# Loading the first keys' weights by rows and ordering the head of a fused attention and Mish kernel anew

## The chip, the cores and the metric

The kernel runs on one core of one Trainium2 chip. The metric is the time of one execution in device microseconds. All times below are microseconds unless marked ns.

## The reference, cut to what matters

```python
def reference(A_x, A_wqkv, A_w_phi, A_wo, B_x, B_w1, B_b1, B_w2):
    def _A_ref(x, wqkv, w_phi, wo):
        B, S, D = x.shape                       # 1, 2048, 512
        H = 32; Dh = D // H                     # Dh = 16
        qkv = (x @ wqkv).reshape(B, S, 3, H, Dh).transpose(2, 0, 3, 1, 4)
        q, k, v = qkv[0], qkv[1], qkv[2]
        pq = jnp.einsum("bhsd,hdf->bhsf", q, w_phi)
        pk = jnp.einsum("bhsd,hdf->bhsf", k, w_phi)
        phi_q = jnp.concatenate([_softmax(pq), _softmax(-pq)], axis=-1)
        phi_k = jnp.concatenate([_softmax(pk), _softmax(-pk)], axis=-1)
        kv = jnp.einsum("bhsf,bhsd->bhfd", phi_k, v)
        z  = jnp.einsum("bhsf->bhf", phi_k)
        num = jnp.einsum("bhqf,bhfd->bhqd", phi_q, kv)
        den = jnp.einsum("bhqf,bhf->bhq", phi_q, z)[..., None] + 1e-6
        return (num / den).transpose(0, 2, 1, 3).reshape(B, S, D) @ wo
    def _B_ref(x, w1, b1, w2):                  # w1: 512 x 1792
        h = jnp.einsum("bsd,df->bsf", x, w1) + b1
        sp = jnp.log1p(jnp.exp(-jnp.abs(h))) + jnp.where(h > 0, h, 0)
        return jnp.einsum("bsf,fd->bsd", h * jnp.tanh(sp), w2)
    x = A_x
    xn = _layernorm(x, axis=-1)
    return x + _A_ref(xn, A_wqkv, A_w_phi, A_wo) + _B_ref(xn, B_w1, B_b1, B_w2)
```

All tensors are bf16. The work is one layer normalisation of 2048 tokens, a linear attention with a learned feature map per head, and a two-layer Mish network, both added to the input.

## The kernel before, in words

The 2048 tokens are 16 tiles of 128, in four groups of four. `w_phi` is folded into the projection weights, so that one matmul of the normalised tokens with the folded weights gives the softmax logits at once. For the keys this fold happens at the very start, in the part here called the head. Everything is issued by one list of steps, `STEPS`, in which each step is a name with arguments: `@3` names a PSUM bank, and `a`, `v`, `p` name ScalarE (ACT), VectorE (DVE) and GpSimd (POOL). Each engine takes its own instructions in the order of the list and waits only for what its operands need. Weights and tokens are loaded by DMAs of SP's queue, two small tensors by ACT's.

The steps of the head are these (tile i of the first group, row block kt of the keys' weights):

- `LS i`, `RS i`, `AZ i`, `TP i`, `TC i`: statistics of token tile i on DVE; its reciprocal root on ACT (two activations, L597 and L598) or POOL (L171 and L172); the normalised tile `xn` on DVE (L176); its transposes on the tensor engine (PE) into `ptr` (L609); and the copy of these to `xnT` (L628).
- `TW kt`, `TK kt`: row block kt of the keys' weights `wkp` is transposed on PE, four blocks of 128 by 128, as plain matmuls with the identity into an fp32 bank `ptw` (L616), and copied to `wT` (L622). Only blocks 0 and 1 go this way; blocks 2 and 3 come already turned, by one DMA transpose out of HBM (L523).
- `WB`: the feature weights `wsrc`, which a DMA of 32-byte pieces lays out, are multiplied with a mask `block` into the block-diagonal `Wbd` on DVE (L568).
- `F0 kt`, `FD kt`: four matmuls of `wT` with `Wbd` into `pfold` (L151), and the copy back to `wkp` (L160).
- `LP i`: logits of token tiles 0 and 1, eight matmuls of 512 columns that take the row blocks in order (L244).
- `PB`, `CB`: the bias turned on PE (L577) and copied on DVE (L669). `KM` builds another mask on DVE (L563). `AM` loads ACT's table for Mish (L139).

Ahead of the steps PE gets twelve warm-up matmuls of ones (L554), nine of 512 columns and three of 128. Behind `LP` come `V t` (values, L229), `VC t` (their copy), `L s i` and `LC s i` (logits of a tile and their copy), `H u` and `M u` (a block of hidden units and its Mish, L263 and L274), `E`, `X`, `S`, `R`, `N`, `A` (softmaxes and accumulation), `LN g` and `AP g k` (normalisation of later groups), `DX g` and `DW i` (later loads).

Of the kernel before, what the change touches and what calls it, by code (L numbers as in the profile page):

```python
# [8 lines left out]
BF16 = mybir.dt.bfloat16  # L9
# [53 lines left out]
def kernel(  # L63
# [13 lines left out]
    P = 128  # L77
# [15 lines left out]
    wphi_v = A_w_phi.rearrange("(j i) a b -> (i a) j b", j=4)  # L93
# [18 lines left out]
    wsrc = wts.tile([P, 4, DH], BF16, name="wsrc")  # L112
    wv = wts.tile([P, KT, D], BF16, name="wv")
# [8 lines left out]
    ident = consts.tile([P, P], BF16, name="ident")  # L122
    mhalf = consts.tile([P, TPG], FP32, name="mhalf")
# [9 lines left out]
    tables = ["natural_log_exp_and_others"]  # L133
# [388 lines left out]
    nc.sync.dma_start(wkp[:, 0:2, :], wqkv_v[:, 0:2, D : 2 * D])
    nc.sync.dma_start_transpose(  # L523
        out=wT_of[0][:, :, 2 * P : 4 * P], in_=A_wqkv[2 * P : 4 * P, D : 2 * D]
    )
# [3 lines left out]
    nc.sync.dma_start(x_sb[:, 2:4, :], x_v[:, 2:4, :])
    nc.sync.dma_start(wv[:], wqkv_v[:, :, 2 * D : 3 * D])  # L530
# [14 lines left out]
    nc.gpsimd.memset(mhalf[:], -0.5)  # L545
    nc.gpsimd.memset(eps[:], 1e-5)
# [20 lines left out]
    def weights_by_block():  # L567
        nc.vector.tensor_tensor(  # L568
            out=Wbd[:].rearrange("p j (h e) -> p j h e", h=8),
            in0=block[:, None, :, :].to_broadcast([P, 4, 8, 16]),  # L570
            in1=wsrc[:, :, None, :].to_broadcast([P, 4, 8, 16]),
            op=ALU.mult,
        )
# [19 lines left out]
    def first_root(i, on):  # L593
        _, mv, rstd = ln_of[0]
        r = rstd[:, i : i + 1]
        if on == "a":
            nc.scalar.activation(r, mv[:, i, 1:2], ACT.Ln, bias=eps[:])  # L597
            nc.scalar.activation(r, r, ACT.Exp, scale=-0.5)  # L598
        else:
            root(r, mv[:, i : i + 1, :])  # L600
# [12 lines left out]
    def turn_keys(kt, b):  # L613
        ptw = pf_of["w", kt] = bank(b, "ptw")
        for j in range(4):
            nc.tensor.matmul(  # L616
# [104 lines left out]
```

## Time and profile before

| | |
|---|---|
| median of 3 runs | 173.61 (173.58 to 173.72) |
| the profiled execution's own time | 173.62 |
| its span, first to last instruction | 171.9 |
| PE busy | 168.3 (98%) |
| DVE busy | 146.0 (85%) |
| ACT busy | 122.2 (71%) |
| POOL busy | 7.9 (5%) |
| mean granted TensorE clock | 1.000 |

Durations and starts in the profile are those of the one profiled execution, counted from the span's start. A row of a timeline gives the start, the time until the last instruction of the row ends, engine, line, operation, output and inputs, and how many such instructions follow each other. In matmul rows the ends are modelled and neighbouring matmuls overlap, so the pace of PE is read from the distance of starts. `PEld` is the loading of weights into PE, and `SPq` and `ACTq` are the instructions that issue DMAs. The granted clock is the share that the throttle grants; it was 1.00 in every slice. The landing time of a DMA counts from the start of its issue.

### The profile page before, as it was taken

The page shows a single profiled execution, that of the slowest core. Times are in us where ns is not written, and L with a number is a line of the kernel's source. Part 1 is how long each engine was busy: PE and PEld are TensorE (multiplying, and loading weights), DVE is VectorE, ACT ScalarE, POOL GpSimd, SP SyncE. Part 2 cuts the span into 40 slices and gives each one's busy share as a digit, 9 for nine tenths or more (in the row PEclk, how much of TensorE's full clock was granted, in tenths as well). Part 3 has the DMA queues.
Part 4 walks back from the last instruction along what each step waited for, and adds up shares of the span by engine and source line. Part 5 has one row for each costly group of instructions (what it writes and reads, how often), then busy time and mean ns, then how long its engine had stood idle before and what let it go on. Part 6 is the DMA issues. An engine that isn't in the chain of part 4 may idle for free.

```text
span 171.9 us, 2743 instructions
## 1 busy us (share of the span) xinstructions
PE 168.3 (98%) x1047; PEld 82.5 (48%) x1047; DVE 146.0 (85%) x226; ACT 122.2 (71%) x196; POOL 7.9 (5%) x23
## 2 busy tenths in 40 slices
PE   8999999999999999999999999999999999999993
PEld 3754444444445544454445644544444444554452
DVE  3769998999899999999989999899799998884333
ACT  2778899976998979799978989978282792432200
POOL 4122102300000000000000000000000000000000
PEclk9999999999999999999999999999999999999999
DMA  4997199686064000000000194309345628778641
GB/s 119 299 374 253 33 217 356 147 162 126 4 115 129 0 4 0 0 0 0 4 0 0 40 111 97 63 15 142 91 107 110 150 59 190 155 161 206 91 124 61
DMA packets 46297, 18.55 MB, mean 108 GB/s; under 512 B 38092, under 2 KB 46284, under 8 KB 46284
## 3 DMA queue, kind: packets, MB, share of 16 engines
q1 hardware_dynamic: 45584, 18.26, 45.8%
q10 hardware_dynamic: 700, 0.12, 0.4%
q8 instruction: 8, 0.13, 0.3%
q14 instruction: 5, 0.04, 0.1%
HBM read 7.10 MB, written 2.10 MB: 53 GB/s over the span
## 4 chain that ended last, share of the span: by engine, by line
PE 98%; DVE 0%; issue 0%
PE ph L263 28%; PE po L497 28%; PE pl L229 14%; PE po L504 8%; PE pv L229 8%; PE warm L554 3%; PE pnd L452 2%; PE pkv L421 2%; PE pl L244 1%; PE pwide L229 1%; PE pfold L151 1%; PE ptw L616 1%; PE ptr L609 1%; PE pfold L203 0%; DVE x_sb L511 0%; PE pb L577 0%
## 5 line engine op out<-in xcount | busy, mean ns | idle before, releaser
L497 PE MATMUL po<-w_sb,acts 128*128 128x512 bf16 (+2 forms) x238 | 50.8, 366 | 0.0
L263 PE MATMUL ph<-xnT,w_sb 128*128 128x512 bf16 x224 | 50.1, 379 | 0.0
L274 ACT ACTIVATE acts<-ph,b1f 128x512 bf16<-128x512 f32 x56 | 35.9, 694 | 5.4 <-PE ph L263 5.4
L340 DVE TENSOR_REDUCE s<-e 128x128 f32<-128x2048 bf16 x16 | 36.1, 2277 | 0.5 <-ACT e L323 0.5
L263 PEld LDWEIGHTS <-w_sb 128*128 128x128 bf16 x224 | 21.7, 98 | 25.9 <-issue 0.3
L497 PEld LDWEIGHTS <-acts 128*128 128x128 bf16 x238 | 22.1, 98 | 23.6
L323 ACT ACTIVATE e<-e 128x2048 bf16<-128x2048 bf16 x16 | 30.4, 1917 | 0.0
L229 PEld LDWEIGHTS <-xnT 128*128 128x128 bf16 x184 | 17.6, 98 | 20.3 <-issue 0.2
L511 DVE TENSOR_TENSOR x_sb<-po,x_sb 128x512 bf16<-128x512 f32 (+2 forms) x17 | 11.0, 656 | 8.4 <-PE po L504 8.4
L504 PE MATMUL po<-wqk,xnT 128*128 128x512 bf16 (+2 forms) x68 | 15.6, 366 | 0.0
L229 PE MATMUL pl<-wqk,xnT 128*128 128x512 bf16 x64 | 15.6, 379 | 0.0
L229 PE MATMUL pv<-wv,xnT 128*128 128x512 bf16 x64 | 15.4, 379 | 0.0
L287 ACT CAST p_sb<-pl 128x512 bf16<-128x512 f32 x21 | 11.9, 590 | 4.1 <-PE pl L229 4.0
L467 ACT COPY ds<-pnd 128x32 f32<-128x32 f32 x16 | 2.9, 183 | 16.5 <-PE pnd L452 16.5
L139 ACT ACT_TABLE_LOAD x10 | 12.8, 1283 | 0.2
L298 DVE TENSOR_TENSOR m<-m 128x512 bf16<-128x512 bf16 (+1 forms) x32 | 11.5, 358 | 1.1
L229 PE MATMUL pl<-wkp,xnT 128*128 128x512 bf16 x48 | 11.5, 379 | 0.0
L165 DVE BATCH_NORM_STATS2 stats<-x_sb 128x6 f32<-128x512 bf16 x16 | 10.1, 678 | 1.3 <-DMA x_sb<-in_A_x_dram 1.3
L298 DVE TENSOR_TENSOR m<-p_sb 128x1024 bf16<-128x1024 bf16 x16 | 10.9, 682 | 0.1
L307 DVE TENSOR_TENSOR e<-p_sb,m 128x2048 bf16<-128x2048 bf16 x8 | 9.8, 1225 | 0.4 <-PE pkv L421 0.2
L374 DVE TENSOR_TENSOR e<-e,r 128x2048 bf16<-128x2048 bf16 x8 | 9.6, 1219 | 0.6 <-ACT r L349 0.5
L307 DVE TENSOR_TENSOR e<-m,p_sb 128x2048 bf16<-128x2048 bf16 x8 | 9.8, 1226 | 0.3
(73 smaller groups left out, 134.0 us busy)
## 6 DMA issues: line engine op xcount, KB each, us to landing
w_sb<-in_B_w_dram SPq DMA_DIRECT2D x4, 896.0 KB, 8.0
out_dram<-x_sb SPq DMA_DIRECT2D x15, 128.0 KB, 2.0
x_sb<-in_A_x_dram SPq DMA_DIRECT2D x3, 512.0 KB, 8.0
wv<-in_A_wqkv_dram SPq DMA_DIRECT2D x1, 512.0 KB, 5.1
wqk<-in_A_wo_dram SPq DMA_DIRECT2D x1, 512.0 KB
x_sb<-in_A_x_dram SPq DMA_DIRECT2D x2, 128.0 KB, 2.1
wkp<-in_A_wqkv_dram SPq DMA_DIRECT2D x1, 256.0 KB, 3.5
x_sb<-in_A_x_dram SPq DMA_DIRECT2D x1, 256.0 KB, 3.5
```

The source lines that it names most:

```text
L139: nc.scalar.preload_act_table_set(name)
L229: nc.tensor.matmul(pp, lhsT=xnT[:, t, kt, :], rhs=w(kt), start=(kt == 0), stop=(kt == KT - 1),)
L263: nc.tensor.matmul(ph_of[u][:], lhsT=w1_sb[:, kt, f * P : (f + 1) * P], rhs=xnT[:, g * TPG : (g + 1) * TPG, kt, :], start=(kt == 0), stop= ...
L274: nc.scalar.activation(acts[:, f, g * 512 : (g + 1) * 512], ph_of.pop(u)[:], ACT.Mish, bias=b1f[:, f : f + 1])
L287: copy(p_of[s][:, i, :], pl_of.pop((s, i)))
L298: nc.vector.tensor_tensor(out=m[:], in0=src[:, :, 0:half], in1=src[:, :, half : 2 * half], op=op)
L307: nc.vector.tensor_tensor(out=e_of[s][:].rearrange("p t j l c -> p (t j) l c")[:, :, pl, :].rearrange("p t (c e o) -> p t c e o", e=8, o=2 ...
L323: nc.scalar.activation(v, v, ACT.Exp)
L340: nc.vector.reduce_sum(t[:], pair(s, k).rearrange("p t j l (c e) -> p (t j l c) e", e=16), axis=AX.X)
L497: nc.tensor.matmul(po_of[t, c.stop][:, c], lhsT=acts[:, f, t * P : (t + 1) * P], rhs=w2_sb[:, f, c], start=(f == 0), stop=False,)
L504: nc.tensor.matmul(po_of[t, c.stop][:, c], lhsT=oT_of[t // 2][:, t % 2 * 4 + j, :], rhs=wo_sb[:, j, c], start=False, stop=(j == 3),)
L511: nc.vector.tensor_tensor(out=y, in0=po_of.pop((t, c.stop))[:, c], in1=y, op=ALU.add)
```

## The change

- The keys' weights come as three natural loads of one row block each (`D wn01`, `D wn12`, `D wn23`), 128 KB each, and one block, the last, by a DMA transpose (`D wu3`). So `TW` and `TK` are done for blocks 0, 1 and 2. `TW` is now PE's transpose into a bf16 bank.
- The feature weights are loaded by rows in pieces of 128 bytes into `wraw`, as the first transfer of ACT's queue. The new step `WX` spreads them on PE, 16 matmuls of 16 columns with slices of a selection matrix `sel`; `WC` copies the result to `wsrc` on ACT; `WB` runs on POOL.
- The warm-ups are steps of the list, `AW n` with n columns. There are thirteen: eleven, 3392 columns in all, stand ahead of `WX`, and two of 64 columns between `TW 0` and `TW 1`.
- Some memsets of constants move from POOL to DVE, and POOL builds `sel`, which borrows the memory of a tile that is used much later.
- The order of the steps from the start to `H 13` is another; from there on it is the same. In the new order the copies of folds 0, 1 and 2 go to ACT and that of fold 3 to DVE, `PB` stands just ahead of the first logits, tile 3 is normalised ahead of tile 2, and the Mish steps begin after more of the H steps.

```diff
 STEPS = """
-KM; LS 0; RS 0 p; LS 1; RS 1 a; DX 2; PB @0; AZ 0; AZ 1; TW 0 @1; TW 1 @2; TP 0 @3; TP 1 @4; TK 0 a;
-TK 1 a; WB; F0 0 @5; FD 0 a; F0 1 @1; TC 0 v; F0 2 @2; F0 3 @3; FD 2 a; TC 1 v; FD 1 v; FD 3 a; LP i
-@4,5; LS 2; LS 3; RS 2 a; LC 0 0 a; V 1 @1; RS 3 p; AZ 2; TP 2 @2; TC 2 a; VC 1 a; AM; V 0 @3; LC 0
-1 v; AZ 3; CB; TP 3 @4; TC 3 v; L 0 2 @5; LC 0 2 a; H 0 @0; M 0; L 0 3 @2; LC 0 3 a; H 1 @1; M 1; H
...
+D x001 s; D phi a; D x011 s; D b1 a; D wn01 s; D wn12 s; TL; D wn23 s; D wu3 s; D x022 s; D wv s; D
+w10007 s; D x044 s; D w10714 s; AW 512; AW 512; AW 512; AW 512; AW 256; AW 256; LS 0; RS 0 a; AW 64;
+AW 64; AW 128; LS 1; AW 64; AW 512; WX @4; TW 0 @3; AW 64; AW 64; TW 1 @1; AZ 0; WC a; RS 1 a; TK 0
+v; TW 2 @4; WB p; AZ 1; TK 1 a; TP 0 @3; TK 2 v; F0 0 @0; FD 0 a; TP 1 @1; F0 1 @4; TC 0 v; FD 1 a;
+TC 1 v; F0 3 @2; F0 2 @3; FD 2 a; FD 3 v; LS 3; PB @0; RS 3 a; LS 2; AZ 3; LP i @5,1; RS 2 p; CB; LC
+0 0 a; V 1 @3; TP 3 @2; LC 0 1 v; AZ 2; V 0 @5; TC 3 a; TP 2 @4; VC 0 a; L 0 3 @1; TC 2 v; H 4 @4;
+KM; LC 0 3 a; L 0 2 @5; H 2 @2; LC 0 2 a; VC 1 v; LN 1; AM; H 1 @1; M 4; H 3 @5; H 0 @0; M 2; E 0 0;
...
-    wphi_v = A_w_phi.rearrange("(j i) a b -> (i a) j b", j=4)
+    wraw = wts.tile([P, 4 * DH], BF16, name="wraw")
+    sel = kvm[:].rearrange("p k c -> p (k c)")[:, 0 : 4 * P + 4]
...
-    nc.sync.dma_start(wkp[:, 0:2, :], wqkv_v[:, 0:2, D : 2 * D])
-    nc.sync.dma_start_transpose(
-        out=wT_of[0][:, :, 2 * P : 4 * P], in_=A_wqkv[2 * P : 4 * P, D : 2 * D]
+        elif what[:2] == "wn":
+            k = slice(int(what[2]), int(what[3]))
+            q.dma_start(wkp[:, k, :], wqkv_v[:, k, D : 2 * D])
+        elif what[:2] == "wu":
+            k = slice(int(what[2]) * P, (int(what[2]) + 1) * P)
+            q.dma_start_transpose(out=wT_of[0][:, :, k], in_=A_wqkv[k, D : 2 * D])
...
+        elif what == "phi":
+            q.dma_start(wraw[:], A_w_phi.rearrange("h (c a) b -> (h c) (a b)", c=4))
...
+    nc.gpsimd.affine_select(
+        out=sel, in_=sel, pattern=[[1, 4 * P + 4]], compare_op=ALU.not_equal,
+        fill=1.0, base=-3, channel_multiplier=-4,
     )
...
-    for n in (512,) * WARM + (P,) * SHORT:
-        dummy(n)
...
-    def weights_by_block():
-        nc.vector.tensor_tensor(
+    def spread(b):
+
+        pf_of["x"] = bank(b, "pspread")
+        for j in range(4):
+            for a in range(4):
+                nc.tensor.matmul(
+                    pf_of["x"][:, j * DH : (j + 1) * DH],
+                    lhsT=sel[:, j * P + 3 - a : (j + 1) * P + 3 - a],
+                    rhs=wraw[:, a * DH : (a + 1) * DH],
+                    start=(j == 0 and a == 0), stop=(a == 3), skip_group_check=True,
+                )
+
+    def weights_by_block(on):
+        {"v": nc.vector, "p": nc.gpsimd}[on].tensor_tensor(
...
     def turn_keys(kt, b):
-        ptw = pf_of["w", kt] = bank(b, "ptw")
+        ptw = pf_of["w", kt] = bank(b, "ptw", BF16)
         for j in range(4):
-            nc.tensor.matmul(
-                ptw[:, j * P : (j + 1) * P], lhsT=wkp[:, kt, j * P : (j + 1) * P], rhs=ident[:],
-                start=True, stop=True,
+            nc.tensor.transpose(
+                ptw[:, j * P : (j + 1) * P], wkp[:, kt, j * P : (j + 1) * P], ident[:]
             )
```

109 lines of the change are left out of this document (59 added, 50 removed).

## The prediction

> **What bounds the kernel now.** I read the page first: busy times and the chain that ended last.
>
> ```profile
> span 171.9 us, 2743 instructions
> ```
> ```profile
> PE 98%; DVE 0%; issue 0%
> ```
>
> PE carries 98% of the chain, so time comes only from fewer or earlier matmuls. A busy PE need not be useful, so the second view is the timeline of PE alone over the first microseconds, and the third the chain in order of time.
>
> ```profile
> 0.83 4.32 PE L554 MATMUL warm<-const-bfloat16-1.0 128*128 128x512 bf16 x12 [0.83 <-PEq L705]
> 5.08 0.19 PE L577 MATMUL pb<-ident,b1b 14*128 14x14 bf16 x1
> 5.25 1.03 PE L616 MATMUL ptw<-ident,wkp 128*128 128x128 bf16 x8
> 6.08 0.76 PE L609 MATMUL ptr<-ident,xn 128*128 128x128 bf16 x8
> 6.67 1.19 PE L151 MATMUL pfold<-Wbd,wT 128*128 128x128 bf16 x16
> 7.74 1.92 PE L244 MATMUL pl<-wkp,xnT 128*128 128x512 bf16 x8
> 9.49 1.03 PE L229 MATMUL pv<-wv,xnT 128*128 128x512 bf16 x4
> 10.35 0.22 PE L609 MATMUL ptr<-ident,xn 128*128 128x128 bf16 x1
> ```
> ```profile
> 14.41 11.22 PE ph L263 x52
> ```
> ```profile
> 74.74 1.02 PE pkv L421 x32
> ```
> ```profile
> 2.06 0.15 PEld L554 LDWEIGHTS <-const-bfloat16-1.0 128*128 128x128 bf16 x1 [0.28 <-issue]
> 2.49 0.15 PEld L554 LDWEIGHTS <-const-bfloat16-1.0 128*128 128x128 bf16 x1 [0.28 <-issue]
> ```
>
> Real work starts at 5.25; before it are only warm-ups. Starts, not durations, give the pace. A warm-up of 512 columns takes 0.43 (2.06 to 2.49), a steady matmul 11.22/52 = 0.216. Of 128 columns, the keys' transposes take 0.83/8 = 0.104, the folds 1.07/16 = 0.067 with a wait among them. So PE runs at half pace at first; the eight token transposes, 0.59 together, fit about three at 0.107 and five at 0.056, which puts the change of pace near 6.35. From 7.74 on, eight matmuls take 1.75 and four 0.86: PE is dense, and it stays so in the chain of waits. So the change is worth what it moves the first logits (7.74 to 9.49) and the V and transposes right behind them.
>
> The fourth view, the timelines of the other engines, tells what releases them.
>
> ```profile
> 2.94 0.69 DVE L165 BATCH_NORM_STATS2 stats<-x_sb 128x6 f32<-128x512 bf16 x1 [0.35 <-DMA x_sb<-in_A_x_dram]
> 3.67 0.18 DVE L167 BATCH_NORM_AGGREGATE mv<-stats 128x2 f32<-128x6 f32 x1
> 3.77 0.66 DVE L165 BATCH_NORM_STATS2 stats<-x_sb 128x6 f32<-128x512 bf16 x1
> 4.46 0.18 DVE L167 BATCH_NORM_AGGREGATE mv<-stats 128x2 f32<-128x6 f32 x1
> 4.87 0.85 DVE L176 TENSOR_SCALAR xn<-x_sb,mv,rstd 128x512 bf16<-128x512 bf16 x2 [0.23 <-POOL rstd L172]
> 5.63 0.42 DVE L568 TENSOR_TENSOR Wbd<-block,wsrc 128x512 bf16<-128x512 bf16 x1
> 6.65 0.75 DVE L628 COPY xnT<-ptr 128x512 bf16<-128x512 bf16 x2 [0.60 <-PE ptr L609]
> 7.45 0.69 DVE L160 CAST wkp<-pfold 128x512 bf16<-128x512 f32 x1
> 8.06 0.68 DVE L165 BATCH_NORM_STATS2 stats<-x_sb 128x6 f32<-128x512 bf16 x1
> ```
> ```profile
> 9.67 0.38 DVE L176 TENSOR_SCALAR xn<-x_sb,mv,rstd 128x512 bf16<-128x512 bf16 x1
> ```
> ```profile
> 4.74 0.29 ACT L597 ACTIVATE rstd<-mv,eps 128x1 f32<-128x1 f32 x1 [1.54 <-DVE mv L167]
> 5.07 0.20 ACT L598 ACTIVATE rstd<-rstd 128x1 f32<-128x1 f32 x1
> 5.89 1.07 ACT L622 CAST wT<-ptw 128x512 bf16<-128x512 f32 x2 [0.62 <-PE ptw L616]
> 7.10 1.65 ACT L160 CAST wkp<-pfold 128x512 bf16<-128x512 f32 x3
> ```
> ```profile
> 1.71 0.43 SPq L522 DMA_DIRECT2D wkp<-in_A_wqkv_dram  x1
> 2.18 1.33 SPq L523 DMA_TRANSPOSE wT<-in_A_wqkv_dram  x1
> 3.56 0.58 SPq L529 DMA_DIRECT2D x_sb<-in_A_x_dram  x1
> 4.18 0.46 SPq L530 DMA_DIRECT2D wv<-in_A_wqkv_dram  x1
> ```
> ```profile
> wv<-in_A_wqkv_dram SPq DMA_DIRECT2D x1, 512.0 KB, 5.1
> x_sb<-in_A_x_dram SPq DMA_DIRECT2D x2, 128.0 KB, 2.1
> wkp<-in_A_wqkv_dram SPq DMA_DIRECT2D x1, 256.0 KB, 3.5
> ```
> ```profile
> wsrc<-in_A_w_phi_dram ACTq DMA_DIRECT2D x1, 16.0 KB, 3.9
> wT<-in_A_wqkv_dram SPq DMA_TRANSPOSE x1, 4.1
> ```
>
> The old start is set by `wkp` (1.71 + 3.5 = 5.2). From there the path is transposes, ACT's copy (5.89), folds (6.67), ACT's copy of fold 0 (7.10 to 7.69), first logits 7.74.
>
> **The change part by part.**
>
> *Loads.* The keys' rows come as three loads of 128 KB, issued at about 1.71, 2.14 and 2.57. By the 128 KB row they land at 3.8, 4.2 and 4.7; by the 256 KB row at up to 6.1. I take the first. The DMA transpose, now one block, is issued near 3.0, so with 4.1 it lands by 7.1, probably sooner with half the bytes. SP reaches `wv` at 3.0 + (0.67 to 1.33) + 0.58 = 4.2 to 4.9; with 5.1 it lands at 9.3 to 10.0. The bytes ahead are the same, so I take 9.3. `DX 2` moves in the list but keeps its place in SP's queue: nothing, as no SP instruction lies between. The feature weights are now the first transfer of ACT's queue, from 0.8: 2.1 to 3.9 gives 2.9 to 4.7; in pieces of 128 bytes instead of 32 I take the lower end.
>
> *Warm-ups and the spread of feature weights, on PE's path.* Ahead of the spread stand 3392 columns of warm-ups, at 0.43 per 512, from 0.83 to about 3.65. The spread adds 16 matmuls of 16 columns. No row shows these at half pace: below, the 1.02/32 = 0.032 of a 65-column matmul at full pace; above, the 0.104 of 128 columns. So 0.5 to 1.7; I take 0.05 each, 0.8, since few columns are nearer to the first row, doubled in part. It ends at 4.45.
>
> *Transposes.* Twelve instead of eight: `TW 0` 4.45 to 4.88, two warm-ups to 4.99, `TW 1` to 5.42, `TW 2` to 5.85, then `TP 0` to 6.28, all at 0.107. `AZ 0` starts at 4.65, behind the second statistics (ACT's root, 0.1 after 3.85 and 0.53 long, is ready at 4.5), so `TK 0` runs 5.13 to 5.55 and frees `TP 0`'s bank in time. The copies read bf16 now and go to DVE, where two such copies took 0.75 (L628), at most 0.42 each. The waits this adds: `TK 0` waits for PE with `AZ 1` behind it on DVE, and the feature weights' copy waits on ACT with `RS 1` behind it. `AZ 1` so ends near 6.0, and `TP 1`, which needs it, comes after `F0 0` anyway.
>
> *Feature weights' product.* The spread's result reaches ACT at 4.72. Its copy is at least 0.20 (L598, one element) and at most 0.59 (512 elements); 0.21 for 64 elements. POOL, with nothing but `RS 2` queued behind, then does the product that took DVE 0.42 (L568).
>
> ```profile
> 1.58 0.75 POOL L540 TENSOR_SCALAR_AFFINE_SELECT block<-block 128x128 bf16<-128x128 bf16 x2
> ```
>
> POOL has no 512-element product in the trace. One of two selects over 128 elements takes about 0.34, so 512 take up to 1.36; with a second input at most 2.7; DVE's 0.42 is the other end. I take 1.36: `Wbd` at 6.34. The Trainium skill (GPSIMD Engine Reference, 4.1 Engine selection) says that two-input elementwise work is about twice as slow there as on VectorE. By that, an estimate of 0.84, `Wbd` would be ready at 5.8 and PE, at 6.28, would set the fold; the end would move by less than 0.1.
>
> *Folds to logits.* `F0 0` starts at 6.36. Before, its copy began 0.43 after the fold and lasted 0.59: 6.79 to 7.38. `PB`, now here and in the same bank, waits for that copy and takes 0.17 (5.08 to 5.25), so the logits start at 7.60. The three copies on ACT end within 1.65, at 8.44, just ahead of the third pair of matmuls at 8.46. Logits end 7.60 + 1.75 = 9.35, 0.14 sooner than before.
>
> *Behind them.* The next steps are `V 1`, 9.35 to 10.21, and `TP 3`, which needs `AZ 3`. DVE gets to it only after `FD 3`: PE does `TP 1` and `F0 1` from 6.58, `F0 3` from 7.02, and 0.43 later, at 7.45, `FD 3` starts and takes 0.69, to 8.14. Before, the two statistics and what waits between them took from 8.06 to 9.67; 1.61 again gives 9.75, `AZ 3` 0.38 more, and PE's transposes 0.1 later, at 10.23. `RS 3` on ACT, 0.63 after the first statistics at about 9.0, is not later than DVE. So PE waits 0.02, and `TP 3` starts 0.12 before the 10.35 of its like. From there the order is transposes, V, transposes, logits, as before.
>
> *Elsewhere.* `KM` and the memsets lie in DVE's idle time; the table load keeps its place; the new order of H and M starts M later by one logits copy and a later table load, but PE has five hidden blocks in other banks then. If that cover fails, PE waits for one ACT step, 0.69 at most.
>
> Sum: spread, transposes and product move the logits by -0.14, the wait for `AZ 3` gives +0.02. The profiled run took 173.62, 1.7 beyond its span, and the median of the runs is 173.61, so the sum goes from 173.6. Forecast 173.5. About 0.2%, 0.35 us, is what a measurement here can tell from no change.
>
> **Rivals.**
>
> *The fast pace comes later (slower).* PE turned fast 5.5 after its first matmul, with nothing but plain matmuls and warm-ups nearly all that time. Now most of what follows 3.65 is small matmuls and transposes. If these count too little, and 5.5 is needed again from 4.45, PE turns at 9.95. Folds and transposes from 6.36 go at 0.107, the logits start at 8.67 and do three matmuls at 0.43 and five at 0.216: end 11.0, 1.5 later, 175.1. It decides when PE is still slow at the first logits. Against it: eight transposes were among the last 1.1 before the turn, as plain matmuls. The Trainium skill (TensorE: Matmul & The Clock Gate, Part 4: PE-mode transpose) says that transposes do not count as busy for the clock gate in the same way; this speaks for it, and the trace cannot test it, because `ptw` used plain matmuls. Chance 0.22.
>
> *POOL's product or the feature weights are late.* At 2.7 `F0 0` starts at 7.7; with landing at 4.7 instead of 3.65 it starts 1.0 later. Either gives about +1.2, 174.8. Chance 0.14.
>
> *DVE and PE both gain.* If the spread takes 0.5 and the product 0.42, and PE turns fast by 4.5, `F0 0` starts at 5.85, logits near 7.1, ending at 8.85; `wv` must then land by 8.8, which needs 4.6 instead of 5.1. That is -0.64, 173.0. Against it: the wait for `wv` already stood just before 9.49.
>
> ```profile
> 9.36 0.10 PEld L229 LDWEIGHTS <-xnT 128*128 128x128 bf16 x1 [0.20 <-DMA wv<-in_A_wqkv_dram]
> ```
>
> Chance 0.22.
>
> **How the numbers follow.** Forecast, within 0.35 of before: 0.42. Faster 0.22. Slower 0.22 + 0.14 = 0.36. Its own range, from the spread (0.5 to 1.0) and the product (0.84 to 1.7), is 173.3 to 173.9. The range for 8 in 10 must take in most of both other sides: 172.9 to 175.1.
>
> **What would show it.** Right: spread about 0.8 long ending near 4.45, `Wbd` near 6.3, logits from 7.6, `TP 3` near 10.2 with `AZ 3` ending just before it. The clock rival: logits 0.43 apart. The product: folds waiting for POOL. The gain: logits before 7.2 and no wait at `V 1` or `TP 3`. I am wrong if a wait of PE later than 14 appears.

## The result, and the profile after

| | before | after |
|---|---|---|
| median | 173.62 (173.11 to 174.29, 14 runs) | 174.94 (173.8 to 176.7, 14 runs) |
| ratio, 95% interval | | 1.0067 [1.0039, 1.0095] |
| profiled execution | 173.62, span 171.9 | 173.99, span 172.3 |

The kernel became slower by 0.7%. Medians are over all executions, while the ratios leave out executions more than 1.5% above the quickest of their kernel and weigh all others, so a ratio is not the quotient of two medians. The profiled execution after is one of its quickest, only 0.37 above before's. So it is read beside a second execution of the same kernel (`a_again`), whose 174.97 is near the median.

The chain of what ended last, on the page of after:

```profile
PE 93%; DMA 3%; SPq 2%; issue 0%; DVE 0%
```

It was 98% PE before. The 5% for DMA and SP's queue lie in the first 9.5 us: the start is now held by a transfer. PE's timeline of after (start, time, engine, line, operation, count, idle time before it and its end):

```profile
3.60 0.60 PE L586 MATMUL pspread<-wraw,kvm 128*128 128x16 bf16 x16
4.32 0.40 PE L643 MATMUL ptw<-ident,wkp 128*128 128x128 bf16 x4
...
5.25 0.38 PE L636 MATMUL ptr<-ident,xn 128*128 128x128 bf16 x4
5.92 0.38 PE L152 MATMUL pfold<-Wbd,wT 128*128 128x128 bf16 x4 [0.29 <-POOL Wbd L594]
...
7.28 1.90 PE L245 MATMUL pl<-wkp,xnT 128*128 128x512 bf16 x8
9.53 1.04 PE L230 MATMUL pv<-wv,xnT 128*128 128x512 bf16 x4 [0.35 <-DMA wv<-in_A_wqkv_dram]
10.40 0.39 PE L636 MATMUL ptr<-ident,xn 128*128 128x128 bf16 x4
```

The logits start 0.46 sooner than before (7.28, 7.74), `V 1` 0.04 later (9.53, 9.49): in this execution the whole gain goes into a wait for `wv`. SP's issues and the landing of `wv` show why, POOL's row belongs to the wait at 5.92:

```profile
3.13 1.29 SPq L533 DMA_TRANSPOSE wT<-in_A_wqkv_dram  x1
...
5.10 0.46 SPq L527 DMA_DIRECT2D wv<-in_A_wqkv_dram  x1
```
```profile
wv<-in_A_wqkv_dram SPq DMA_DIRECT2D x1, 512.0 KB, 4.4
```
```profile
4.60 1.27 POOL L594 TENSOR_TENSOR Wbd<-block,wsrc 128x512 bf16<-128x512 bf16 x1 [1.63 <-ACT wsrc L695]
```

One transposed block takes SP 1.29 to issue, two took 1.33; with three natural loads ahead of it, `wv` is issued at 5.10 instead of 4.18 and is there at 9.5 instead of 9.3.

Behind the head PE falls back twice. The first place is the hidden blocks behind the second pair of wide copies; PE's and ACT's timelines of before, then of after:

```profile
29.79 1.03 PE L229 MATMUL pwide<-wkp,xnT 128*128 128x512 bf16 x4
30.66 1.67 PE L263 MATMUL ph<-xnT,w_sb 128*128 128x512 bf16 x7
```
```profile
11.87 1.28 ACT L139 ACT_TABLE_LOAD   x1
...
29.25 1.84 ACT L274 ACTIVATE acts<-ph,b1f 128x512 bf16<-128x512 f32 x3
```
```profile
29.84 1.03 PE L230 MATMUL pwide<-wkp,xnT 128*128 128x512 bf16 x4
30.90 1.46 PE L264 MATMUL ph<-xnT,w_sb 128*128 128x512 bf16 x6
```
```profile
15.11 1.28 ACT L140 ACT_TABLE_LOAD   x1
...
29.59 1.84 ACT L275 ACTIVATE acts<-ph,b1f 128x512 bf16<-128x512 f32 x3
```

Four matmuls took 0.87 before, and 1.06 pass now. ACT does the same steps 0.34 later; the new order of H and M, which puts the table load for Mish (`AM`) at 15.11 instead of 11.87, is the likely reason, and `a_hm` below tests the order. (The order is new a little beyond `H 13`: the Mish steps `M 5` and `M 8` also stand behind it.) The second of the three activations ends at about 30.9, when the next hidden block starts; that it frees this block's bank is read from the list, not from a wait in the profile.

The second place is an attention product (`Q`) near 157, which needs a DMA transpose of the exponentials. PE in before, after and the second execution of after:

```profile
157.17 0.42 PE L452 MATMUL pnd<-kvm,qT 128*128 128x68 bf16 x8
```
```profile
157.42 0.42 PE L453 MATMUL pnd<-kvm,qT 128*128 128x68 bf16 x8
```
```profile
158.39 0.43 PE L453 MATMUL pnd<-kvm,qT 128*128 128x68 bf16 x8 [0.74 <-DMA qT<-e]
```

Against before, the second execution is 0.1 late at `V 1` (9.61), 0.3 behind 30.9 and 1.2 at this product, which is all of its loss but 0.1. So the largest part of this execution's loss, 0.9, is this one wait, and most experiments ask what makes that transpose late. It isn't there in every execution: the first profile of after has none.

### The profile page after: what moved, and what is told of

It reads as the page before. It is cut to its first block, busy times and chain, and to the rows that moved or that the text cites. A ratio compares the mean times of both kernels' runs of the same rounds, so it can differ in the third digit from the quotient of the medians.

```text
span 172.3 us, 2791 instructions
## 1 busy us (share of the span) xinstructions
PE 167.7 (97%) x1068; PEld 82.5 (48%) x1068; DVE 147.7 (86%) x233; ACT 121.1 (70%) x197; POOL 8.4 (5%) x19
## 4 chain that ended last, share of the span: by engine, by line
PE 93%; DMA 3%; SPq 2%; issue 0%; DVE 0%
PE ph L264 28%; PE po L498 28%; PE pl L230 14%; PE pv L230 8%; PE po L505 8%; DMA wv<-in_A_wqkv_dram 3%; PE pnd L453 2%; PE pkv L422 2%; PE pwide L230 1%; SPq L525 1%; SPq L530 1%; SPq L533 1%; PE ptr L636 0%; PE pfold L204 0%; DVE x_sb L512 0%
## 5 line engine op out<-in xcount | busy, mean ns | idle before, releaser
L275 ACT ACTIVATE acts<-ph,b1f 128x512 bf16<-128x512 f32 x56 | 35.1, 692 | 4.8 <-PE ph L264 4.7
```

The lines of the kernel that those rows point to most:

```text
L275: nc.scalar.activation(acts[:, f, g * 512 : (g + 1) * 512], ph_of.pop(u)[:], ACT.Mish, bias=b1f[:, f : f + 1])
```

## Experiments

Medians, with the ratio to the kernel before measured beside each (the kernels were measured in five groups, each with its own before of 173.40 to 173.71):

| run | what it is | median | ratio, 95% |
|---|---|---|---|
| `a_again` | after, unchanged | 175.15 | 1.0095 [1.008, 1.011] |
| `a_rows4` | after, all four blocks natural | 175.25 | 1.0098 [1.0079, 1.0117] |
| `a_plain` | after, `TW` as plain matmuls | 174.2 | 1.0049 [1.0029, 1.0068] |
| `b_few` | before, 6 fewer warm-ups | 174.53 | 1.0061 [1.0042, 1.0081] |
| `b_pad` | before, 21 more PE matmuls | 173.63 | 1.0004 [0.9987, 1.002] |
| `a_pad30` | after, 30 more PE matmuls | 174.79 | 1.0075 [1.005, 1.01] |
| `a_hm` | after, old order of H and M | 175.02 | 1.0066 [1.0041, 1.0091] |
| `a_wv` | after, `wv` loaded sooner | 176.15 | 1.0149 [1.0127, 1.017] |
| `a_al` | after, no tile moved by 128 bytes | 174.43 | 1.0045 [1.0029, 1.006] |
| `a_alhm` | `a_al` with old order of H and M | 174.04 | 1.0026 [1.0004, 1.0047] |
| `b_128` | before, tiles moved by 128 bytes | 173.77 | 1.0003 [0.9988, 1.0018] |
| `b_128pad` | both `b_128` and `b_pad` | 173.83 | 1.0025 [1.0002, 1.0048] |
| `b_f` | before, 30 more PE matmuls | 174.18 | 1.0037 [1.0024, 1.005] |
| `b_128f` | both `b_128` and `b_f` | 173.97 | 1.0028 [1.0014, 1.0041] |
| `c_x2a` | `a_alhm`, tiles 2 and 3 by ACT's queue | 174.79 | 1.0069 [1.0043, 1.0095] |
| `c_ta` | `a_alhm`, turned block by ACT's queue | 176.45 | 1.0167 [1.0137, 1.0196] |
| `c_w1` | `a_alhm`, w1's first load split | 173.59 | 1.0036 [1.0009, 1.0062] |

**The parts of the head: `a_again`, `a_rows4`, `a_plain`, `b_few`.**

> The changed kernel as it is, for its spread and a second profile. Theory 1 (pace): the moment at which PE goes from half to full pace differs from execution to execution, and the changed head has little to fall back on when it is late. Then the times spread again over 2 us or more, 173.8 to 176.5, and if the profiled execution is above 174.8 its first logits start about 0.43 apart instead of 0.216. Theory 2 (values' weights): the loss is the late load of wv alone. Then every execution has the same wait at V 1, the spread stays near that of the kernel before (1.2 us) and a second profile looks like the first, with first logits from 7.3 and V 1 at 9.5.

The loss is real. These five executions vary little (174.95 to 175.19), less than the fourteen of the result (173.8 to 176.7), and the second profile does not look like the first: it has no wait for `wv`, and one at 157. Neither theory foresaw that.

```diff
-D wn23 s; D wu3 s;
+D wn23 s; D wn34 s;
-TK 2 v; F0 0 @0;
+TK 2 v; TW 3 @2; TK 3 a; F0 0 @0;
```

> All four row blocks natural: the DMA transpose of the last block is gone, TW 3 and TK 3 are added (four PE transposes, one copy on ACT ahead of FD 0). SP issued the transpose for 1.29 us; a natural load takes 0.43, so wv is issued at about 4.2 instead of 5.1. Theory 2: wv lands 0.9 earlier, V 1 starts at about 9.2 at the latest instead of 9.53, and the fastest and the median times fall by 0.3 to 0.4 alike. Theory 1: the fastest times fall by 0.3, since the wait is real, but the spread of 2 to 3 us above them stays, and the median stays above 174.2.

The same time as after. The fourth natural block lands near 7.0 and `TW 3` waits 0.95 for it; `V 1` comes at 10.56, 0.95 behind `a_again`, yet the whole is hardly slower, because the wait at 157 shrinks to 0.22. So the end of this kernel does not simply follow its head. The fall of 0.3 to 0.4 that an earlier `wv` was to bring did not come.

```diff
-        ptw = pf_of["w", kt] = bank(b, "ptw", BF16)
+        ptw = pf_of["w", kt] = bank(b, "ptw")
         for j in range(4):
-            nc.tensor.transpose(
-                ptw[:, j * P : (j + 1) * P], wkp[:, kt, j * P : (j + 1) * P], ident[:]
+            nc.tensor.matmul(
+                ptw[:, j * P : (j + 1) * P], lhsT=wkp[:, kt, j * P : (j + 1) * P], rhs=ident[:],
+                start=True, stop=True,
             )
```

> The keys' weights turned by plain matmuls with the identity into an fp32 bank, as before the change, and otherwise the changed kernel. Theory 1 with transposes not counting as work for the pace: the spread falls to that of the kernel before and the median to about 173.9. Theory 1 without that: spread and median stay (174.9), with up to 0.3 more for the slower copies (0.69 instead of 0.41 on DVE, twice). Theory 2: no change but the slower copies, hidden behind the wait for wv. The Trainium skill (TensorE: Matmul & The Clock Gate, Part 4: PE-mode transpose) says that transposes do not count as busy in the same way; the run tells whether that matters here.

The head did not get quicker (`V 1` at 9.86, 0.29 of it for `wv`), so the rival of a late fast pace finds no support. In after's profile PE was at full pace by the first transposes: they passed at 0.06 each from 4.32 on. `a_again` turned fast only near 6.6, and still had `V 1` at 9.61. The median, though, is 0.95 below `a_again`, nearer to the 173.9 of the theory that transposes don't count than to the 174.9 of the other. Its profile has no wait at 157: the first of the last pair of transposes landed in 3.2, the second in 4.8. The code fetch of which the experiments below tell is recorded at 156.6 here, just as the first landed; but in `a_hm` it is recorded at 156.75, and there the first was late. So a few tenths decide, and why this execution was spared is not settled.

```diff
-WARM, SHORT = 9, 3
+WARM, SHORT = 3, 3
```

> The kernel before with three long warm-ups instead of nine, nothing else: PE idles from about 2.4 to 5.1, and real work still starts at 5.25. Theory 1: the pace depends on how PE was used in the microseconds before, so PE turns fast only some us after 5.25; each us of slow pace costs half of it, so the median rises by 1 to 2.5 us, to 174.6 to 176.1, with first logits 0.43 apart in the profile. Theory 2, and any theory in which only loads and the order of steps matter: nothing changes, 173.6.

With six warm-ups fewer the same steps run at half pace until the logits, and `V 1` starts 0.78 later than in before:

```profile
10.27 1.03 PE L229 MATMUL pv<-wv,xnT 128*128 128x512 bf16 x3
```

So nearly all of `b_few`'s 0.9 is pace. After, with `V 1` at 9.53 and 9.61, does not have this loss.

**The order: `a_hm`, `a_wv`.**

```diff
-L 0 3 @1; TC 2 v; H 4 @4; KM; LC 0 3 a; L 0 2 @5; H 2 @2; LC 0 2 a; VC 1 v; LN 1; AM; H 1 @1; M 4;
...
+AM; L 0 3 @1; LC 0 3 a; TC 2 v; H 0 @0; M 0; L 0 2 @5; LC 0 2 a; VC 1 v; KM; H 1 @1; M 1; H 2 @4;
...
```

> The changed kernel with the order of hidden blocks and Mish as before from the first logits copies to H 13, so that ACT's table for Mish is loaded at 12.3 instead of 15.1. Expected: ACT ends its first ten Mish at 22.9 instead of 23.3 and PE's wait of 0.2 at 30.7, behind the second wide logits, is gone; the median falls by 0.2. PE's instructions are the same in number, so by theory F the late waits for qT stay and the median is 174.7. If the order of H and M were the main loss, it would fall to 173.8.

The 0.2 is gone as expected (wide copies at 30.30, hidden blocks at 31.16, 0.86 apart). But `V 1` came at 9.39 here, and the time came back at the next transfer, w1:

```profile
13.02 1.04 PE L264 MATMUL ph<-xnT,w_sb 128*128 128x512 bf16 x4 [0.42 <-DMA w_sb<-in_B_w_dram]
```

The median hardly moved, because the transpose at 157 is late in this kernel too (0.82). So the old order removes the wait at 30.9; it changes the whole order of H and M, so it does not show that the table load alone was the reason.

```diff
-D wu3 s; D x022 s; D wv s;
+D wu3 s; D wv s; D x022 s;
-V 1 @3; TP 3 @2; LC 0 1 v; AZ 2; V 0 @5; TC 3 a;
+V 1 @3; V 0 @5; TP 3 @2; LC 0 1 v; AZ 2; TC 3 a;
```

> The changed kernel with wv loaded ahead of token tiles 2 and 3, and V 0 ahead of TP 3 on PE. Theory W: the earlier first logits (7.28) are worth nothing because wv lands at 9.5; with wv issued at 4.5 it lands by 8.8 and V 1 starts right behind the logits, 9.1, V 0 at 9.9. Tiles 2 and 3 then land near 9.4 instead of 7.9, so that TP 3 cannot start before about 11.2 and PE waits there instead: from L 0 3 on all is as late as in the changed kernel or up to 0.5 later. That would show that the bytes ahead of the second logits bound the head. If instead only the order of issue were at fault, L 0 3 would start 0.4 earlier (11.3 instead of 11.7).

`V 1` no longer waits (9.25), but the tiles 2 and 3 come later, and ACT, where their root stands ahead of a logits copy, holds `V 0`:

```profile
11.63 1.02 PE L230 MATMUL pv<-wv,xnT 128*128 128x512 bf16 x4 [1.35 <-ACT p_sb L288]
```

`L 0 3` comes at 13.55, 1.8 later than in after, where up to 0.5 was expected: the wait came at `V 0` and not at `TP 3`, as the theory had it.

**The code fetch: `b_pad`, `a_pad30`.** The records of transfers hold packets of 16 KB on a queue called "instruction", the last of them at 159.4 in before, 156.6 in after and 155.7 in `a_again`. They are taken to be PE's code, which fits that more matmuls move them ahead. Both experiments cut warm-up columns into more matmuls, so that PE has more instructions for the same work.

```diff
-WARM, SHORT = 9, 3
+WARM, SHORT = 2, 31
```

> The kernel before with its 4992 warm-up columns cut into 33 matmuls instead of 12 (two of 512, 31 of 128): the same time of PE, 21 matmuls with their weight loads more, as many more as the changed kernel has. Theory F (code fetch): PE's instructions come by DMA in pieces of 16 KB; more of them ahead move every later fetch about 3 us forward, from 159.4 to about 156.5, into the last transposes of the queries, which land late. Then the head stays as before (logits at 7.7, V 1 at 9.5), but the last landing of qT rises from 3.0 to 4 or more, a wait of PE for qT appears near 157 in the profile or in some of the runs, and the median rises by 0.3 to 1.0, to 173.9 to 174.6. Theory H (head): the loss comes from the head alone; with the head's work unchanged the time stays at 173.6.

```diff
-AW 512; AW 512; AW 512; AW 512; AW 256; AW 256; LS 0;
+AW 128; AW 128; AW 128; AW 128; AW 64; AW 64; AW 64; AW 64;
...
+AW 64; AW 64; AW 64; AW 64; LS 0;
```

> The changed kernel with its first six warm-ups (2560 columns) cut into 36, four of 128 and 32 of 64: 30 matmuls more, the same columns. Theory F: the fetch that now falls at 156.6 moves by about 60/256 of the 19 us between fetches, to about 152, between two groups of transposes; qT lands in 2.8 to 3.2 again, no wait for qT at 158, and the median falls from 175.0 to about 174.1. Theory H: nothing changes, or it gets slower by what the small warm-ups cost, and the median stays at 174.9 or above.

In `b_pad` the last packet moved to 156.1, as theory F said, but the loss that it foresaw did not come: only the second of the pair landed late (4.4). In `a_pad30` the packet moved to 154.7 and not to 152, so it still met the pair; the first transpose landed in 4.4, and the product near 157 was 0.14 late. Most of this kernel's loss was another, a wait of 0.58 for w1 at 13.15. By themselves these two left open whether the fetch matters.

**128 bytes: `a_al`, `b_128`, `b_128pad`, `a_alhm`.** The DMA transposes of the exponentials land later after, those of the scaled sums that lie in `wkp` sooner. The view of DMA issues (size, then median time to landing), before and after:

```profile
qT<-e SPq DMA_TRANSPOSE x16, 2.8
...
xnT<-wkp SPq DMA_TRANSPOSE x4, 3.2
```
```profile
qT<-e SPq DMA_TRANSPOSE x16, 3.2
...
xnT<-wkp SPq DMA_TRANSPOSE x4, 2.7
```

The tile `wraw`, which the change adds, takes 128 bytes of each partition and moves every tile behind it. In the built kernels the first buffer of the exponentials starts at byte 181,760 of a partition before, a multiple of 256, and at 181,888 after; `wkp` at 59,776, 128 off a multiple, and at 59,904, a multiple. `a_al` puts the raw feature weights elsewhere, `b_128` adds an idle tile of that size to before.

```diff
-    wraw = wts.tile([P, 4 * DH], BF16, name="wraw")
+    wraw = acts[:, FT - 1, S - 4 * DH : S]
```

> The kernel after, but the raw feature weights lie in a corner of the activations' buffer that is written much later, not in a tile of their own. So no tile behind them is moved by 128 bytes: the exponentials and their turned copies start at a multiple of 256 bytes again, as before. Theory of the shifted tiles: a DMA transpose of the exponentials lands in 2.8 again instead of 3.2, one of the scaled sums in 3.2 instead of 2.7, the last attention products no longer wait for their transposes, and the median comes down by 0.7 to 1.3, to 173.7 to 174.2. Theory of PE's code (its last 16 KB fetch alone, now at 155 to 157, makes the transposes late): the waits stay, 174.7 to 175.2. Theory of the head (the turn of the clock): also 174.7 to 175.2, with the loss at the first V already.

> The same, and the order of the H and M steps of the first group as in the kernel before. Shifted tiles: 0.2 below the kernel beside it, because the wait ahead of the first hidden block after the second pair of wide copies is gone, unless the first hidden blocks wait for w1's landing near 12.5 to 13 (0.4): 173.5 to 174.2. Other theories: 174.7 to 175.2.

```diff
     wsrc = wts.tile([P, 4, DH], BF16, name="wsrc")
+    pad = wts.tile([P, 4 * DH], BF16, name="pad")
```

> The kernel before, with an unused tile of 128 bytes a partition where the change puts the raw feature weights: all later tiles move by 128 bytes, no instruction changes. Shifted tiles: transposes of the exponentials land in 3.2 instead of 2.8, of the scaled sums in 2.7 instead of 3.2. The last code fetch stays at 159.4, behind the last transposes of exponentials, so by this theory together with the fetch the time stays within 0.3 of 173.6; by the shifted tiles alone it is 0.4 to 1.0 more. Other theories: 173.6 and no change of any landing.

> The kernel before with both: the unused 128 bytes, and the same 4992 warm-up columns in 33 matmuls instead of 12, which alone changed nothing (173.63) and moves the last 16 KB fetch of PE's code from 159.4 to 156.1. Shifted tiles and fetch together: slow transposes meet the fetch, a product near 157 waits 0.2 to 0.9 for its transpose, 174.0 to 174.6. Fetch alone or tiles alone: 173.6, no wait. Head: 173.6.

The same two rows in `a_al` and in `b_128`:

```profile
qT<-e SPq DMA_TRANSPOSE x16, 2.8
...
xnT<-wkp SPq DMA_TRANSPOSE x4, 3.1
```
```profile
qT<-e SPq DMA_TRANSPOSE x16, 3.2
...
xnT<-wkp SPq DMA_TRANSPOSE x4, 2.8
```

The landing follows the 128 bytes in both kernels and both directions: with the source at a multiple of 256 bytes it comes about 0.4 sooner. The targets of these transposes move on and off a multiple together with the sources, so the target could be the reason. The other four transposes of scaled sums tell the two apart. Their source, in `wv`, starts 64 bytes off a multiple before (25,664) and 192 off after (25,792), while their target `xnT` comes onto a multiple (80,256, then 80,384); before and after, the same row:

```profile
xnT<-wv SPq DMA_TRANSPOSE x4, 3.1
```

The target alone changes nothing, so it is the source. The Trainium skill (DMA: Bandwidth & Descriptors, How a descriptor splits into AXI transactions) says that a read which does not start at a multiple of 256 bytes fetches from the boundary below and pays for bytes it does not use; these rows agree.

In time, `a_al` is 0.7 below `a_again`, the least fall that the theory asked, though its 174.43 lies above the 174.2 of the forecast and its interval overlaps that of the result's after. No product waits at 157, but the fetch meets the second of the pair (5.2), and the product of that one is 0.2 late:

```profile
159.84 0.43 PE L453 MATMUL pnd<-kvm,qT 128*128 128x68 bf16 x8
```

In before it starts 1.98 behind the one at 157.17, here 2.17 behind its like. In `a_alhm` the 0.2 at 30.9 is gone too (30.08, 30.94), and the first hidden block waits 0.4 for the landing of w1 (12.80). `b_128` is unchanged, as the theory together with the fetch asked. `b_128pad`, with both, was to lose 0.4 to 1.0; it lost 0.1 by the medians and 0.4 by the ratio (0.0 to 0.8), with one execution at 175.61. In its profile the last pair landed in 3.3 and 4.5; the fetch met the second, whose product comes 2 us later, so nothing waited.

**The meeting: `b_f`, `b_128f`.** So the fetch was put into the packets of the first of the pair.

```diff
-    for n in (512,) * WARM + (P,) * SHORT:
+    for n in (P,) * 36 + (64,) * 6:
```

> The kernel before, with its 4992 warm-up columns in 42 matmuls (36 of 128, 6 of 64) instead of 12. 21 more matmuls moved the last code fetch of 16 KB from 159.4 to 156.1 and cost nothing; 30 more should put it near 154.6, in the middle of the packets of the transpose on which the attention product near 157 waits. That transpose lands in 2.8 to 3.0 and has 4.3 of room. Theory of the meeting (a transpose whose packets meet the fetch lands 1 to 2 later): landing 4.0 to 5.0, a wait of 0 to 0.7 near 157, median 173.6 to 174.3. Theory that the fetch doesn't matter: 173.6, no wait.

> The same 42 warm-ups and the unused 128 bytes that make transposes of the exponentials land in 3.2. The room is 1.1 here instead of 1.5. Theory of the meeting: a wait of 0.3 to 1.1 near 157, median 174.0 to 174.8, and more than beside it without the 128 bytes. Fetch doesn't matter: 173.7.

The last pair of transposes of the exponentials, issued near 153 (landing, smallest, median and largest): before, `b_pad`, `b_f`, `a_again`, `a_al`, from the view of the tile in this stretch.

```profile
DMA to landing us min/median/max: 2.8/2.9/3.0
```
```profile
DMA to landing us min/median/max: 3.0/3.7/4.4
```
```profile
DMA to landing us min/median/max: 4.5/4.8/5.0
```
```profile
DMA to landing us min/median/max: 4.8/5.0/5.2
```
```profile
DMA to landing us min/median/max: 2.8/4.0/5.2
```

And the transfers of 152 to 157 in 40 slices (busy tenths, then GB/s), before and `b_f`, whose fetch of 16 KB is at 154.55:

```profile
DMA  0000039999999996499999994103999999932998
GB/s 16 0 0 0 0 66 219 223 211 217 215 213 201 178 199 134 103 240 272 281 285 289 293 256 84 19 0 90 256 291 291 291 289 289 246 56 57 287 328 279
```
```profile
DMA  0049999999996499999050000000000000399999
GB/s 0 0 82 213 231 211 219 209 213 201 184 193 123 105 233 268 260 160 25 0 131 0 0 0 0 0 0 0 8 6 10 8 10 8 68 274 289 289 265 293
...
q8 instruction: 1, 0.02, 1.2%
```

In `b_f` the transfer stands in the middle: the slice with 131 GB/s is the fetch, and around it hardly anything else moves for 1.9 us. Then the product waits:

```profile
157.53 0.43 PE L452 MATMUL pnd<-kvm,qT 128*128 128x68 bf16 x8 [0.58 <-DMA qT<-e]
```

So before loses 0.6 without any other change than that its warm-ups are cut into 30 more matmuls. The head is not the reason: in this profile `V 1` starts at 9.10, sooner than in before. The records of all the profiles here agree. Of the transposes of exponentials whose landing is known, 188 have no packet of 16 KB between issue and landing, and the slowest of them took 3.4; 42 took over 3.5, and every one of these has such a packet. That the meeting of fetch and transpose makes this wait is shown.

`b_128f` was to lose more than `b_f`; it lost about as much (0.38 and 0.59, intervals overlapping). The 128 bytes are no condition; they take 0.4 of the room. In `a_hm` and `a_alhm`, which differ by them alone, the fetch is recorded at the same 156.75, and the first of the pair lands in 5.3 with them and in 2.8, issued 0.2 sooner, without. Of the seven profiles of after and its variants with the 128 bytes, four have the product near 157 late (0.74, 0.82, 0.22, 0.14), three not; of the five without them, none.

**The loads: `c_x2a`, `c_ta`, `c_w1`.**

```diff
-D wn23 s; D wu3 s; D x022 s; D wv s;
+D wn23 s; D wu3 s; D wv s;
-LS 0; RS 0 a;
+LS 0; RS 0 a; D x022 a;
```

> The kernel after with the raw feature weights in the activations' buffer and the old order of H and M (174.04 so far), and the load of token tiles 2 and 3 issued by ACT behind the first root, near 4.4, instead of by SP ahead of wv. SP then issues wv near 4.5 instead of 5.1 and w1 near 5.0 instead of 5.6. Theory that the landings of wv and w1 hold the head: V 1 right behind the logits, near 9.2 to 9.4, no wait of the first hidden block, 173.6 to 173.8. If the loads are held by bytes and not by their issue: wv lands at 9.3 to 9.8 as ever, 174.0.

```diff
-D b1 a;
+D wu3 a;
-D wn23 s; D wu3 s; D x022 s;
+D wn23 s; D x022 s;
-LS 0; RS 0 a;
+LS 0; RS 0 a; D b1 a;
```

> As the kernel before this one in the list, but it is the turned block of keys' weights that ACT issues (first behind the feature weights; the table load and the biases' load come behind it), and SP issues tiles 2 and 3 near 3.1, wv near 3.8, w1 near 4.3. Landings held by issue: wv by 8.8, no wait at V 1 nor at the first hidden block, 173.4 to 173.7; it costs ACT's first root up to 0.3, which the wait for the product hides in part. Held by bytes: 174.0.

Both came out slower than either theory asked (174.79 and 176.45, where 174.0 was the highest forecast). `wv` issued at 4.47 in `c_x2a` lands 5.0 later, at 9.5 again, which fits a hold by bytes; but issued near 5.1 it landed anywhere from 9.05 to 9.81 in these profiles, so one execution does not show it. The profile of `c_x2a` is its quickest execution (173.78) and does not show its usual loss. In `c_ta` the keys' weights land later, as it seems because the loads around them take the bytes, and `TW 0` waits. DMA issues of `c_x2a`, of `c_ta`, and PE in `c_ta`:

```profile
wv<-in_A_wqkv_dram SPq DMA_DIRECT2D x1, 512.0 KB, 5.0
```
```profile
wkp<-in_A_wqkv_dram SPq DMA_DIRECT2D x3, 128.0 KB, 3.7
```
```profile
5.44 0.61 PE L643 MATMUL ptw<-ident,wkp 128*128 128x128 bf16 x4 [1.20 <-DMA wkp<-in_A_wqkv_dram]
```

In after the three landed in 2.4. `c_w1` leaves the bytes ahead of `wv` as they are, and lets the first hidden blocks wait for 512 KB of w1 instead of 896.

```diff
-D w10007 s;
+D w10004 s; D w10407 s;
```

> The kernel after with the raw feature weights in the activations' buffer and the old order of H and M (174.04 so far, first hidden block at 12.80 behind the landing of w1), and w1's first load of seven column blocks (896 KB) split into loads of four and three, so that the first hidden blocks need 512 KB only. Theory that w1's landing holds the first hidden block: no wait there, 12.5 or sooner, and 0.2 to 0.3 below 174.04, 173.7 to 173.9, about the kernel before. Other theories: 174.0.

PE in `a_alhm`, then in `c_w1`:

```profile
12.80 1.04 PE L264 MATMUL ph<-xnT,w_sb 128*128 128x512 bf16 x4 [0.24 <-DVE vext L254]
```
```profile
12.33 1.03 PE L264 MATMUL ph<-xnT,w_sb 128*128 128x512 bf16 x4
```

The first hidden block comes at 12.33 instead of 12.80, without a wait, and no product waits at 157. In `a_alhm` the row names a copy on DVE that ended at the same moment as the load; in `c_w1` that copy ends at 12.69, behind the block's start, so it was the load that held it. The profiled execution took 173.47 and the median is 173.59, against 173.40 of the kernel before beside it. But three of twelve executions took 174.8 to 175.7, where before never passed 174.3, and the ratio, which counts them fully, is 1.0036, no better than that of `a_alhm` (1.0026). So the loss is taken back but for about 0.2 in the usual execution and 0.6 by the ratio; that the split gains time is shown at the block and not in the whole. No version here beats before.

## Why the prediction failed, by its own steps

Forecast 173.5, measured 174.94: outside the forecast's own 173.3 to 173.9, inside the wide range.

*Spread, transposes, product.* Right in kind. The spread took 0.60 (0.8 forecast), `TW 0` began at 4.32 (4.45), POOL's product took 1.27 (1.36) and held `F0 0` by 0.29. The Trainium skill (GPSIMD Engine Reference, 4.1 Engine selection) puts such work on GpSimd at about twice VectorE's time, an estimate of 0.84 here. That is not borne out: 1.27 against 0.42 on VectorE is 3 times. The logits came at 7.28 (7.60), mainly because the product was ready at 5.87 and not at 6.34: its input was there sooner. The keys' loads landed later than forecast (4.28, 4.61 and 4.93 for 3.8, 4.2 and 4.7), and in `a_again` the last two came later still (4.83 and 5.61), so that `TW 1` and `TW 2` waited. PE was at half pace until near 6.6 there, and `V 1` at 9.61 followed the logits without a wait for `wv`.

*`wv`.* The term that was mis-sized: issue 4.2 to 4.9 was forecast, it was 5.10. The upper bound of a transpose's issue (1.33) was the right one, and the natural loads ahead of it end at 3.13. `V 1` was forecast at 9.35 and came at 9.53. The rival "DVE and PE both gain" named the right limit, the landing of `wv`, but asked for it only with logits near 7.1. They take 1.75, so while `wv` lands at 9.5 nothing is gained by logits before 7.7, and the forecast's own 7.60 lay below that. `AZ 3` was ready at 9.89, ahead of `TP 3` at 10.40, so no wait there.

*"Elsewhere".* The step that failed: everything behind the head was put at nothing. It allowed "one ACT step, 0.69 at most" if the cover of the new order of H and M fails, and took nothing; it costs 0.2 at 30.9. And it looked for waits of PE only where a step of the list had moved. The prediction's own sentence, wrong "if a wait of PE later than 14 appears", is what happened, at 30.9 and at 157.

*The rivals on the slow side* gave about the right time (174.8, 175.1) by the wrong mechanism: neither a late turn of pace nor a late product set the end. That the wide range holds the measured time is owed to these two, so it is luck.

What the runs put in their place, in medians over before: after 1.3 to 1.6; without the 128 bytes 0.7; with the old order of H and M as well 0.3; with w1 split 0.2. By the ratios it is 1.2 to 1.6, 0.8, 0.5 and 0.6. The first difference is the late transpose where the traces show it, at 157; how many of the executions have it is not known. The second is 0.2 by the trace and 0.4 by the medians, and the intervals overlap; the third the ratios don't show. Open remain what is left behind these, with the few executions above 174.8, and the low median of `a_plain`.

## What to carry to other kernels

A new tile, even of 128 bytes, moves the addresses of all tiles behind it; keep the sources of DMA transposes at multiples of 256 bytes, or borrow memory that is idle. Here this is worth 0.4 of a landing, and time only where something waits for the landing (`b_128` lost nothing). A change in the number of matmuls moves the code fetches, so look in the transfers of the changed kernel for what they now meet, and in more than one execution. Ahead of a stage that waits for bytes, an earlier matmul is worth nothing: look first for the landing that ends last there, and for the one behind it.

## What the runs showed of the hardware

- DMA transposes of 128 by 1024 bf16 from one on-chip tile to another land in 2.7 to 2.8 when their source starts at a multiple of 256 bytes and in 3.1 to 3.2 when it starts 64, 128 or 192 bytes off (medians of the views of before, after, `a_al` and `b_128`).
- The last code fetch of 16 KB moved from 159.4 to 156.1 with 21 more matmuls and to 154.55 with 30 more. Its place varies by about 1 us between executions of one kernel (156.6 and 155.7 in after). A transpose of the last pair that was late from meeting it landed in 4.2 to 5.3, where 2.8 or 3.2 is usual.
- Issuing a DMA transpose out of HBM takes SP 1.29 for one block of 128 by 512 (after) and 1.33 for two (before).
- PE's pace turned at different times in two executions of one kernel. In both the last warm-up, from 3.2 on, took 0.41 for 512 columns, half pace; 128 columns took 0.056 from 4.4 on in after's profile, and in `a_again` 0.107 until near 6.6.
